# Rounding the cosine's phase by an integer conversion on ScalarE, in a long convolution followed by a gated layer

## Chip, core and metric

The kernel runs on one core of one Trainium2 chip. The metric is the time of one execution on the device in microseconds (us). Several runs of the same kernel are compared by their median.

## What is computed

The reference has two halves. The first is a long convolution along the sequence, for 4 batches of 12480 positions and 128 channels; the second sends every one of the 49920 rows through a layer with 2048 hidden units, whose gate is a cosine.

```python
def _attn_ref(x, v, pos_emb, w1, w2):           # x, v: (4, 12480, 128)
    h_mlp = np.maximum(pos_emb @ w1, 0.0) @ w2
    window = np.exp(-0.01 * np.arange(S))[:, None]
    h_filt = h_mlp * window
    u = x * v
    L = 2 * S
    Uf = np.fft.rfft(u, n=L, axis=1)
    Hf = np.fft.rfft(h_filt, n=L, axis=0)
    y = np.fft.irfft(Uf * Hf[None, :, :], n=L, axis=1)[:, :S, :]
    return (x * y).astype(np.float32)

def _moe_ref(x, w_in, w_out):                   # x: (49920, 128)
    h = x @ w_in                                # (128, 2048)
    g = h * np.cos(h)
    return (g @ w_out).astype(np.float32)       # (2048, 128)
```

All of it is float32; the two weights of the second half arrive as float64.

## The kernel before

**The convolution.** The transform over the sequence is written as matmuls of a two-stage factorisation (96 by 120). For each batch there are five stages: `u` (load x and v, multiply, sums and differences of mirrored positions, into the big buffer `slots`), `f1` (first forward matmuls), `f2` (second forward matmuls and the product with the filter's spectrum), `i1` (first inverse matmuls) and `i2` (second inverse matmuls, then the product with x and a store of the result to DRAM as `zd`). A stage is a generator that yields after every small unit of work, with a number that says how many steps of the second half should go by before the next unit.

**The stage u.** `u_load` issues two DMAs for one group of positions, into tiles `xt` (3 buffers) and `vt` (2 buffers). `u_multiply` (L395) multiplies `xt` by `vt` in two halves of 256 elements in 104 partitions; the engine of each half is chosen by a function that the caller gives. `u_sums` (L401) writes the sum of the halves (on GpSimd) and their difference (on VectorE) into `slots`. There are 30 groups in a batch. The groups of batch b + 1 run inside the stage `i2` of batch b (`inverse_units`), once `i2` has read the places in `slots` that they overwrite. In batch 0's `i2`, a quarter of the multiplications run on GpSimd and the rest on VectorE; in the later ones all run on VectorE. The groups of batch 0 run at the start of the kernel, with a choice of engines of their own.

**The second half.** It runs from about 340 us to the end, woven into the convolution of all later stages. One step is one tile of up to 128 rows by 4 (512 columns) and one of the 16 blocks of 128 hidden units: 98 tiles of rows by 16 blocks, 1568 steps. `moe_up` does the first matmul into the PSUM tile `ph` (TensorE, L743), then `a` = ph / (2 pi) + 1/4 on ScalarE (L746), `k` = a rounded to a whole number on VectorE, by adding and subtracting a large constant (L749), and `f` = a - k on GpSimd (L752). `moe_act`, one step later, does the sine of 2 pi f on ScalarE (`cs`, L757), which is cos(h), and `gt` = ph * cs on VectorE (L759). `moe_down`, four steps later, adds the second matmul into the accumulator `acc` (L768; in every second tile near the end the accumulator is called `cv`). `ph` has 4 PSUM buffers, so the matmul of a step needs the `gt` of four steps before. `a` has 3 buffers, `k` and `f` 2.

Each tile of rows is loaded from `zd` (tile `zb`), turned by four transposes (L126) and copied by ScalarE (`at`, L737). At the end of a tile, ScalarE evicts `acc` (`ot`, L774), four transposes and a copy (`ob`, L783) follow, and SP issues the stores to the output (L794).

**The order.** The schedule is written out by hand: the text of the program decides the order of the instructions on each engine. The main loop goes over the steps; after each step it draws units of convolution until they cover what is owed:

```python
            owed += 1.0
            while owed > 0.0:
                owed -= next(conv, owed)
```

All loads and stores are issued by SP's queue, in the program's order. In the stage `i2` a group's matmuls (L504) use a table `tm` (2 buffers, loaded at L676) and x again (`xs`); the eviction with the product is `zs` on VectorE (L511).

**The weights.** They are converted from the bits of float64 to float32 beside the stages f1 and i1 of batch 0: `convert_units` goes over pieces, `float32_parts` (two activations with a scale among others) and `float32_join` do one.

Of the kernel before, what the change touches and what calls it, by code (L numbers as in the profile page):

```python
# [8 lines left out]

F32 = mybir.dt.float32  # L10
U32 = mybir.dt.uint32
AF = mybir.ActivationFunctionType
ALU = mybir.AluOpType
# [3 lines left out]
P = 128  # L17
BANK = 512
DECAY = -0.01

INV_TWO_PI = 1.0 / (2.0 * math.pi)

TWO_PI = 6.283185

ROUND = 12582912.0

TAPS = 10400

# [2 lines left out]
def kernel(  # L31
# [46 lines left out]
    nc = tc.nc  # L78
# [9 lines left out]
    ODD = 64  # L88
# [12 lines left out]
    UA = 2  # L101
# [7 lines left out]
    dram = ctx.enter_context(tc.tile_pool(name="dram", bufs=1, space=DRAM))  # L109
    hd = dram.tile([N1 // 2, N2, 2, CB, 4], F32, name="hd")  # L110
    zd = dram.tile([NROWS, G, D], F32, name="zd")
    wd = dram.tile([N1 // 2, KE, 2, N2], F32, name="wd")
    td = dram.tile([N2 // G, N1, G, 2, R], F32, name="td")
    wind = dram.tile([D, DFF], F32, name="wind")
    csd = dram.tile([N2, 2, N2], F32, name="csd")
# [10 lines left out]
        nc.tensor.transpose(dst, src, ident[0:n, 0:n])  # L126


    def float32_parts(pool, raw):
        lo, hi = raw[:, :, 0], raw[:, :, 1]  # L130

        power = pool.tile([P, WCOL], U32, name="power", bufs=2)
        nc.vector.tensor_scalar(out=power[:, :], in0=hi, scalar1=20, scalar2=0x7FF,
                                op0=ALU.logical_shift_right, op1=ALU.bitwise_and)
        nc.gpsimd.tensor_scalar(out=power[:, :], in0=power[:, :], scalar1=1023.0 - 127.0,
                                scalar2=0.0, op0=ALU.subtract, op1=ALU.max)
        nc.gpsimd.tensor_scalar(out=power[:, :], in0=power[:, :], scalar1=255.0,
                                scalar2=float(1 << 23), op0=ALU.min, op1=ALU.mult)

        sig = pool.tile([P, WCOL], U32, name="sig", bufs=2)  # L140
        nc.vector.tensor_scalar(out=sig[:, :], in0=hi, scalar1=0xFFFFF, scalar2=0x100000,
                                op0=ALU.bitwise_and, op1=ALU.bitwise_or)
        high = sig[:, :].bitcast(F32)
        nc.scalar.activation(high, sig[:, :], AF.Copy, scale=2.0 ** -20)
        low = pool.tile([P, WCOL], F32, name="low", bufs=1)
        nc.scalar.activation(low[:, :], lo, AF.Copy, scale=2.0 ** -52)
        nc.gpsimd.tensor_tensor(high, high, low[:, :], op=ALU.add)
        return power, high

    def float32_join(dst, raw, power, high):  # L150
# [6 lines left out]
        if dst.space == DRAM:  # L157
# [9 lines left out]
    def convert_units(pool, pieces):  # L167

        raws, half = [], None
        for i in range(len(pieces) + 1):  # L170
            while len(raws) < min(i + 2, len(pieces)):
                raws.append(pool.tile([P, WCOL, 2], U32, name="raw", bufs=3))
                nc.sync.dma_start(raws[-1][:, :, :], pieces[len(raws) - 1][1])
            yield
            if i > 0:
                float32_join(pieces[i - 1][0], raws[i - 1], *half)
            if i < len(pieces):
                half = float32_parts(pool, raws[i])


    class Tables:
# [212 lines left out]
        xt, vt = tiles  # L394
        engine.tensor_tensor(xt[:, half, :], xt[:, half, :], vt[:, half, :], op=ALU.mult)  # L395

    def u_sums(u, tiles, a):
        both = tiles[0][:, :, :].rearrange("p h (n b i) -> p h n b i", n=UA, i=2)
        below, above = both[:, 0, ::-1, :, :], both[:, 1, :, :, :]
        for place, op, e in ((a, ALU.add, nc.gpsimd), (ODD + a, ALU.subtract, nc.vector)):  # L400
            e.tensor_tensor(u[0:R, :, place:place + UA, :].transpose([0, 2, 1, 3]),  # L401
                            below, above, op=op)

# [158 lines left out]
    def u_units(b, bufs, u, engine, side="left"):  # L562

        with tc.tile_pool(name="xv", bufs=bufs, side=side) as pool:
            tiles = {}

            def before(j):
                tiles[j] = u_load(pool, bufs, b, j * UA)

            def after(j, _):  # L570
                for half in range(2):
                    u_multiply(tiles[j], half, engine(j, half))
                    yield
                if j == H // UA - 2:
                    clear_gap(u)
                u_sums(u, tiles.pop(j), j * UA)
                yield

            yield from units(H // UA, U_STEPS, before, lambda j, ps, i: None, after, 3,
                             ahead=bufs - 2)  # L580
# [159 lines left out]
    def moe_up(pool, n, c):  # L740
        m = G * rows_of(n)
        ph = ps_h.tile([P, BANK], F32, name="ph")
        nc.tensor.matmul(ph[:, 0:m], w_in_sb[:, c * P:(c + 1) * P], ats[n][:, 0:m],  # L743
                         start=True, stop=True)
        a = pool.tile([P, BANK], F32, name="a", bufs=3)
        nc.scalar.activation(a[:, 0:m], ph[:, 0:m], AF.Identity,  # L746
                             bias=quarter[:, 0:1], scale=INV_TWO_PI)
        k = pool.tile([P, BANK], F32, name="k")
        nc.vector.tensor_scalar(out=k[:, 0:m], in0=a[:, 0:m], scalar1=ROUND,  # L749
                                scalar2=ROUND, op0=ALU.add, op1=ALU.subtract)  # L750
        f = pool.tile([P, BANK], F32, name="f")
        nc.gpsimd.tensor_tensor(f[:, 0:m], a[:, 0:m], k[:, 0:m], op=ALU.subtract)  # L752
        return ph, f, m

    def moe_act(pool, ph, f, m):
        cs = pool.tile([P, BANK], F32, name="cs")
        nc.scalar.activation(cs[:, 0:m], f[:, 0:m], AF.Sin, scale=TWO_PI)  # L757
        gt = pool.tile([P, BANK], F32, name="gt", bufs=4)
        nc.vector.tensor_tensor(gt[:, 0:m], ph[:, 0:m], cs[:, 0:m], op=ALU.mult)  # L759
        return gt  # L760
# [39 lines left out]
    with tc.manual_schedule():  # L800
        with tc.tile_pool(name="psum", bufs=8, space=PSUM) as psum, \
# [71 lines left out]

            backs = [inverse_units(lambda: bank(), b) for b in range(B)]

            def beside(units, pieces, more=lambda pool: iter(())):
                with tc.tile_pool(name="convert", bufs=1) as pool:
                    convert, other = convert_units(pool, pieces), more(pool)
# [8 lines left out]
            beside(f1_units(bank, slots[0:R, :, :, :], 0.55),  # L887
                   [(wind[:, c], w) for c, w in in_pieces])
# [7 lines left out]
            wpool = ctx.enter_context(tc.tile_pool(name="weights", bufs=1))  # L896
# [10 lines left out]
            beside(i1_units(bank), [(w_out_sb[:, c, :], w) for c, w in out_pieces], some_groups)  # L907
# [97 lines left out]
```

## Time and profile before

| what | value |
|---|---|
| time, median of 3 runs | 3761.64 us (3761.51 to 3764.51) |
| profiled execution, first to last instruction | 3758.9 us; no time of its own stands beside this span |
| TensorE (PE) busy | 3690.6 us, 98% |
| VectorE (DVE) busy | 2773.7 us, 74% |
| ScalarE (ACT) busy | 2508.2 us, 67% |
| GpSimd (POOL) busy | 2557.6 us, 68% |
| mean granted clock of TensorE | 0.995 of full speed |
| x * v on VectorE, L395 | 177 times, 132.6 us, mean 751 ns |
| x * v on GpSimd, L395 | 63 times, 50.5 us, mean 812 ns |
| difference on VectorE, L401 | 120 times, 72.2 us, mean 601 ns |
| sum on GpSimd, L401 | 120 times, 108.8 us, mean 906 ns |

In a group's row of the profile stand the line, the engine, the operation, what is written and read with the shape of one instruction and their number, then the busy time in us and the mean duration of one in ns, and after the next bar the time for which the engine stood idle just before them with what ended it. A line of waits names who waited, what it waited for, the sum in us, how often, and the longest. A line of the timeline has the start and the duration in us; an idle time of the engine before it stands in brackets.

### The profile page before, as it was taken

The numbers are of one execution on the slowest core, as the hardware profiler recorded it, in microseconds if no ns is written. First come the engines' busy times: TensorE is split into PE (matmuls) and PEld (weight loads), VectorE is DVE, ScalarE is ACT, GpSimd is POOL, SyncE is SP. The second block draws the span as 40 slices with busy tenths as digits, with TensorE's granted clock in tenths as the row PEclk, the third lists the DMA queues.
The fourth block names the chain that finished last, engine by engine and source line by source line (L and its number), as shares of the span: only waits on it lengthen the run. The fifth ranks groups of instructions, "written<-read, shape, count | busy, mean of one in ns | idle before, by whom it ended". The sixth has DMA issues, their size and how long they took to land.

```text
span 3758.9 us, 47177 instructions
## 1 busy us (share of the span) xinstructions
PE 3690.6 (98%) x13546; PEld 2110.4 (56%) x13546; DVE 2773.7 (74%) x5586; ACT 2508.2 (67%) x4660; POOL 2557.6 (68%) x2318
## 2 busy tenths in 40 slices
PE   7898999999999999999999999999999999999999
PEld 6777555555566556555565556555566544444444
DVE  8887997687866787788766776788765666666666
ACT  5757776766665557766665567666664677777777
POOL 6666776588845665688745664788644677777776
PEclk9999999999999999999999999999999999999999
DMA  6263551022203650122104530122105200000000
GB/s 167 64 185 107 155 167 33 25 72 79 72 12 91 181 151 12 40 79 77 52 18 128 180 105 21 52 79 76 38 21 172 76 23 17 17 23 18 17 23 13
DMA packets 209499, 276.14 MB, mean 73 GB/s; under 512 B 17111, under 2 KB 146535, under 8 KB 209111
## 3 DMA queue, kind: packets, MB, share of 16 engines
q1 hardware_dynamic: 209239, 273.12, 24.8%
q8 instruction: 109, 1.79, 0.2%
q14 instruction: 151, 1.24, 0.1%
HBM read 193.64 MB, written 79.42 MB: 73 GB/s over the span
## 4 chain that ended last, share of the span: by engine, by line
PE 88%; DVE 3%; POOL 3%; ACT 2%; DMA 2%; issue 1%; SPq 0%; POOLq 0%; DVEq 0%; ACTq 0%
PE ph L743 33%; PE acc L768 28%; PE cv L504 5%; PE cv L768 5%; PE cv L479 4%; PE cv L407 3%; PE cv L448 3%; PE ph L126 2%; POOL f L752 1%; PE ps L407 1%; PE ps L448 1%; DMA tm<-td 1%; DMA wd<-w 1%; ACT cs L757 1%; DVE k L749 1%
## 5 line engine op out<-in xcount | busy, mean ns | idle before, releaser
L752 POOL TENSOR_TENSOR f<-a,k 128x512 f32<-128x512 f32 (+1 forms) x1568 | 1986.2, 1267 | 1060.5 <-DVE k L749 1059.1
L743 PE MATMUL ph<-at,w_in_sb 128*128 128x512 f32 (+1 forms) x3136 | 1599.0, 591 | 3.7 <-DVE gt L759 2.7
L746 ACT ACTIVATE a<-ph,quarter 128x512 f32<-128x512 f32 (+1 forms) x1568 | 1071.2, 683 | 704.8 <-PE ph L743 695.2
L768 PE MATMUL acc<-gt,w_out_sb 128*128 128x512 f32 (+1 forms) x2688 | 1370.3, 591 | 0.0
L759 DVE TENSOR_TENSOR gt<-ph,cs 128x512 f32<-128x512 f32 (+1 forms) x1568 | 1077.3, 687 | 359.9 <-ACT cs L757 341.8
L757 ACT ACTIVATE cs<-f 128x512 f32<-128x512 f32 (+1 forms) x1568 | 981.0, 626 | 366.6 <-POOL f L752 364.3
L749 DVE TENSOR_SCALAR k<-a 128x512 f32<-128x512 f32 (+1 forms) x1568 | 792.9, 506 | 550.7 <-ACT a L746 524.2
L768 PEld LDWEIGHTS acc<-gt,w_out_sb 128*128 128x128 f32 x2688 | 508.4, 189 | 642.8 <-issue 631.9
L743 PEld LDWEIGHTS ph<-at,w_in_sb 128*128 128x128 f32 x3136 | 553.2, 190 | 337.7 <-issue 257.5
L474 POOL TENSOR_TENSOR slots<-slots,t 120x256 f32<-120x256 f32 x384 | 312.9, 821 | 59.9 <-DVE t L467 25.6
L504 PEld LDWEIGHTS cv<-slots,tm 96*104 96x104 f32 x1920 | 238.6, 169 | 106.8 <-issue 85.4
L504 PE MATMUL cv<-slots,tm 96*104 96x128 f32 x1920 | 251.7, 273 | 9.9 <-POOL tm L297 5.0
L768 PE MATMUL cv<-gt,w_out_sb 128*128 128x512 f32 (+1 forms) x448 | 224.5, 583 | 1.0 <-DVE gt L759 1.0
L479 PEld LDWEIGHTS cv<-cs,slots 120*96 120x96 f32 x1536 | 176.7, 167 | 67.2 <-issue 65.2
L479 PE MATMUL cv<-cs,slots 120*96 120x120 f32 x1536 | 183.2, 266 | 0.0
L448 PEld LDWEIGHTS cv<-slots,w 124*120 124x120 f32 x576 | 103.7, 184 | 124.3 <-issue 112.3
L407 PEld LDWEIGHTS cv<-c,slots 104*124 104x124 f32 x768 | 132.6, 192 | 72.2 <-issue 60.0
L448 PE MATMUL cv<-slots,w 124*120 124x256 f32 x576 | 173.0, 380 | 0.0
L407 PE MATMUL cv<-c,slots 104*124 104x192 f32 x768 | 151.8, 327 | 5.4 <-DVE gt L759 3.5
L768 PEld LDWEIGHTS cv<-gt,w_out_sb 128*128 128x128 f32 x448 | 84.9, 190 | 104.8 <-issue 99.5
L489 DVE TENSOR_TENSOR slots<-cv,other 96x240 f32<-96x240 f32 x384 | 133.1, 394 | 1.5 <-ACT other L487 1.4
L395 DVE TENSOR_TENSOR xt<-xt,vt 104x256 f32<-104x256 f32 x177 | 132.6, 751 | 0.6 <-DMA vt<-in_v_dram 0.6
(131 smaller groups left out, 2520.9 us busy)
## 6 DMA issues: line engine op xcount, KB each, us to landing
h<-hd SPq DMA_DIRECT2D x144, 240.0 KB
tm<-td SPq DMA_DIRECT2D x96, 312.0 KB
xt<-in_x_dram SPq DMA_DIRECT2D x120, 208.0 KB
vt<-in_v_dram SPq DMA_DIRECT2D x120, 208.0 KB
xs<-in_x_dram SPq DMA_DIRECT2D x120, 208.0 KB
zd<-zs SPq DMA_DIRECT2D x119, 208.0 KB
zb<-zd SPq DMA_DIRECT2D x96, 256.0 KB
w<-wd SPq DMA_DIRECT2D x144, 116.2 KB
```

The lines of the kernel that those rows point to most:

```text
L407: nc.tensor.matmul(ps[0:KE, i * 2 * N1:(i + 1) * 2 * N1], u[:, b, 0:KE, i], c1[0:u.shape[0], :, :].rearrange("p r k -> p (r k)"), start=Tr ...
L448: nc.tensor.matmul(pi, w[:, i, :], parts[0:KE, :, k], start=True, stop=True)
L474: nc.gpsimd.tensor_tensor(y[:, r], y[:, r], t[:, r], op=op)
L479: nc.tensor.matmul(ps[0:N1, (i * 2 + r) * N2:(i * 2 + r + 1) * N2], parts[0:N2, r, :, b, i], cs[:, r, :], start=True, stop=True)
L504: nc.tensor.matmul(ps[0:R, i * D:(i + 1) * D], t[:, i, r, :], slots[0:N1, :, place, :], start=(r == 0), stop=(r == 1))
L743: nc.tensor.matmul(ph[:, 0:m], w_in_sb[:, c * P:(c + 1) * P], ats[n][:, 0:m], start=True, stop=True)
L746: nc.scalar.activation(a[:, 0:m], ph[:, 0:m], AF.Identity, bias=quarter[:, 0:1], scale=INV_TWO_PI)
L749: nc.vector.tensor_scalar(out=k[:, 0:m], in0=a[:, 0:m], scalar1=ROUND, scalar2=ROUND, op0=ALU.add, op1=ALU.subtract)
L752: nc.gpsimd.tensor_tensor(f[:, 0:m], a[:, 0:m], k[:, 0:m], op=ALU.subtract)
L757: nc.scalar.activation(cs[:, 0:m], f[:, 0:m], AF.Sin, scale=TWO_PI)
L759: nc.vector.tensor_tensor(gt[:, 0:m], ph[:, 0:m], cs[:, 0:m], op=ALU.mult)
L768: nc.tensor.matmul(accs[n][:, 0:m], w_out_sb[:, c, :], gt[:, 0:m], start=(c == 0), stop=(c == NFC - 1))
```

## The change

In each step, `a` is gone. ScalarE adds a constant number of quarter turns to `ph` and writes `k` as an int32, so that its conversion does the rounding. VectorE then forms `f` = (ph + constant) - k, reading `ph` from PSUM again and `k` as an integer. The division by 2 pi is in the first weight, and the factor 2 pi that `gt` then lacks is in the second; both come from the scales of the activations that convert the weights. The constant goes round 0.25, 0.75, -0.25 and -0.75 with the block, and the sign of the sine's scale goes with it. `k` keeps 2 buffers, `f` has 3. The constant tile `quarter` is gone.

The groups of u for batches 1 to 3 multiply on GpSimd alone, and their sum and their difference both run on GpSimd. Those of batch 0 stay as they were.

```diff
+TURNS = ((0.25, 1.0), (0.75, -1.0), (-0.25, -1.0), (-0.75, 1.0))
...
-    def float32_parts(pool, raw):
+    def float32_parts(pool, raw, factor):
...
-        nc.scalar.activation(high, sig[:, :], AF.Copy, scale=2.0 ** -20)
+        nc.scalar.activation(high, sig[:, :], AF.Copy, scale=factor * 2.0 ** -20)
...
-        nc.scalar.activation(low[:, :], lo, AF.Copy, scale=2.0 ** -52)
+        nc.scalar.activation(low[:, :], lo, AF.Copy, scale=factor * 2.0 ** -52)
...
-    def u_sums(u, tiles, a):
+    def u_sums(u, tiles, a, takers):
...
-        for place, op, e in ((a, ALU.add, nc.gpsimd), (ODD + a, ALU.subtract, nc.vector)):
+        for place, op, e in ((a, ALU.add, takers[0]), (ODD + a, ALU.subtract, takers[1])):
...
-                u_sums(u, tiles.pop(j), j * UA)
+                u_sums(u, tiles.pop(j), j * UA, (nc.gpsimd, nc.gpsimd if b else nc.vector))
...
-                      lambda j, half: nc.gpsimd if b == 0 and j % 2 > half else nc.vector,
+                      lambda j, half: nc.gpsimd,
...
-        a = pool.tile([P, BANK], F32, name="a", bufs=3)
-        nc.scalar.activation(a[:, 0:m], ph[:, 0:m], AF.Identity,
-                             bias=quarter[:, 0:1], scale=INV_TWO_PI)
-        k = pool.tile([P, BANK], F32, name="k")
-        nc.vector.tensor_scalar(out=k[:, 0:m], in0=a[:, 0:m], scalar1=ROUND,
-                                scalar2=ROUND, op0=ALU.add, op1=ALU.subtract)
-        f = pool.tile([P, BANK], F32, name="f")
-        nc.gpsimd.tensor_tensor(f[:, 0:m], a[:, 0:m], k[:, 0:m], op=ALU.subtract)
-        return ph, f, m
+        k = pool.tile([P, BANK], I32, name="k")
+        nc.scalar.activation(k[:, 0:m], ph[:, 0:m], AF.Identity, bias=TURNS[c % 4][0])
+        f = pool.tile([P, BANK], F32, name="f", bufs=3)
+        nc.vector.scalar_tensor_tensor(out=f[:, 0:m], in0=ph[:, 0:m],
+                                       scalar=TURNS[c % 4][0], in1=k[:, 0:m], op0=ALU.add, op1=ALU.subtract)
+        return ph, f, m, TURNS[c % 4][1] * TWO_PI
...
-        nc.scalar.activation(cs[:, 0:m], f[:, 0:m], AF.Sin, scale=TWO_PI)
+        nc.scalar.activation(cs[:, 0:m], f[:, 0:m], AF.Sin, scale=scale)
...
-            quarter = wpool.tile([P, 1], F32, name="quarter")
-            nc.vector.memset(quarter[:, :], 0.25)
```

The two calls that convert the weights give `INV_TWO_PI` and `2.0 * math.pi` as the factor.

More of the change, by code (lines that the diff above doesn't have):

```diff
@@ L10 @@
 F32 = mybir.dt.float32
+I32 = mybir.dt.int32
 U32 = mybir.dt.uint32
@@ L165, with convert_units @@
                   for c in range(0, NFC, WCOL // D)]
-    def convert_units(pool, pieces):
+    def convert_units(pool, pieces, factor):
         raws, half = [], None
@@ L177, in convert_units @@
             if i < len(pieces):
-                half = float32_parts(pool, raws[i])
+                half = float32_parts(pool, raws[i], factor)
     class Tables:
@@ L744, in moe_up, with moe_act @@
                          start=True, stop=True)
-        a = pool.tile([P, BANK], F32, name="a", bufs=3)
-        nc.scalar.activation(a[:, 0:m], ph[:, 0:m], AF.Identity,
-                             bias=quarter[:, 0:1], scale=INV_TWO_PI)
-        k = pool.tile([P, BANK], F32, name="k")
-        nc.vector.tensor_scalar(out=k[:, 0:m], in0=a[:, 0:m], scalar1=ROUND,
-                                scalar2=ROUND, op0=ALU.add, op1=ALU.subtract)
-        f = pool.tile([P, BANK], F32, name="f")
-        nc.gpsimd.tensor_tensor(f[:, 0:m], a[:, 0:m], k[:, 0:m], op=ALU.subtract)
-        return ph, f, m
-    def moe_act(pool, ph, f, m):
+        k = pool.tile([P, BANK], I32, name="k")
[4 more added lines that the diff above has]
+        return ph, f, m, TURNS[c % 4][1] * TWO_PI
+    def moe_act(pool, ph, f, m, scale):
         cs = pool.tile([P, BANK], F32, name="cs")
-        nc.scalar.activation(cs[:, 0:m], f[:, 0:m], AF.Sin, scale=TWO_PI)
+        nc.scalar.activation(cs[:, 0:m], f[:, 0:m], AF.Sin, scale=scale)
         gt = pool.tile([P, BANK], F32, name="gt", bufs=4)
@@ L874, with beside @@
             backs = [inverse_units(lambda: bank(), b) for b in range(B)]
-            def beside(units, pieces, more=lambda pool: iter(())):
+            def beside(units, pieces, factor, more=lambda pool: iter(())):
                 with tc.tile_pool(name="convert", bufs=1) as pool:
-                    convert, other = convert_units(pool, pieces), more(pool)
+                    convert, other = convert_units(pool, pieces, factor), more(pool)
                     for i, _ in enumerate(units):
@@ L887 @@
             beside(f1_units(bank, slots[0:R, :, :, :], 0.55),
-                   [(wind[:, c], w) for c, w in in_pieces])
+                   [(wind[:, c], w) for c, w in in_pieces], INV_TWO_PI)
             lpool = ctx.enter_context(tc.tile_pool(name="late", bufs=1))
@@ L903 @@
             w_out_sb = wpool.tile([P, NFC, D], F32, name="w_out_sb")
-            quarter = wpool.tile([P, 1], F32, name="quarter")
-            nc.vector.memset(quarter[:, :], 0.25)
             nc.sync.dma_start(w_in_sb[:, :], wind[:, :])
-            beside(i1_units(bank), [(w_out_sb[:, c, :], w) for c, w in out_pieces], some_groups)
+            beside(i1_units(bank), [(w_out_sb[:, c, :], w) for c, w in out_pieces], 2.0 * math.pi,
+                   some_groups)
         ps_acc = ctx.enter_context(tc.tile_pool(name="ps_acc", bufs=1, space=PSUM))
```

## The prediction

> **What bounds the kernel now.** I read the page first: one engine is busy nearly all the time, and the five operations of a step of the second half stand among the costliest groups.
>
> ```profile
> PE 3690.6 (98%) x13546; PEld 2110.4 (56%) x13546; DVE 2773.7 (74%) x5586; ACT 2508.2 (67%) x4660; POOL 2557.6 (68%) x2318
> ...
> L752 POOL TENSOR_TENSOR f<-a,k 128x512 f32<-128x512 f32 (+1 forms) x1568 | 1986.2, 1267 | 1060.5 <-DVE k L749 1059.1
> ...
> L746 ACT ACTIVATE a<-ph,quarter 128x512 f32<-128x512 f32 (+1 forms) x1568 | 1071.2, 683 | 704.8 <-PE ph L743 695.2
> ...
> L759 DVE TENSOR_TENSOR gt<-ph,cs 128x512 f32<-128x512 f32 (+1 forms) x1568 | 1077.3, 687 | 359.9 <-ACT cs L757 341.8
> L757 ACT ACTIVATE cs<-f 128x512 f32<-128x512 f32 (+1 forms) x1568 | 981.0, 626 | 366.6 <-POOL f L752 364.3
> L749 DVE TENSOR_SCALAR k<-a 128x512 f32<-128x512 f32 (+1 forms) x1568 | 792.9, 506 | 550.7 <-ACT a L746 524.2
> ```
>
> TensorE sets the end. What the other engines do matters only where TensorE stands still for them, so the second view is TensorE's waits from 340 us on, where the steps begin (the 50 us that it idles before that lie in stages whose work does not change).
>
> ```profile
> PE cv L504 <- DMA tm<-td: 4.8, 6, 1.4
> PE cv L407 <- DVE gt L759: 3.5, 3, 1.9
> PE ph L743 <- DVE gt L759: 2.7, 5, 0.8
> PE cv L407 <- DVE slots L417: 1.9, 2, 1.0
> PE cv L768 <- DVE gt L759: 1.0, 2, 0.7
> PE ph L743 <- ACT at L737: 0.6, 1, 0.6
> PE ph L126 <- ACT ot L774: 0.5, 1, 0.5
> ```
>
> Columns: total us, times, longest. The sum is 15.0 us in 20 waits. A 512-column matmul is drawn 0.59 us long while the next follows after 0.43 (pairs start 0.86 apart in the timeline), so each wait lost 0.16 us more than shown: 15.0 + 20 x 0.16 = 18.2 us. The timeline of the second row's longest wait shows one more loss:
>
> ```profile
> 591.51 1.02 PE L768 MATMUL acc<-gt,w_out_sb 128*128 128x512 f32 x2
> ...
> 592.23 0.72 POOL L395 TENSOR_TENSOR xt<-xt,vt 104x256 f32<-104x256 f32 x1
> 593.03 1.30 POOL L401 TENSOR_TENSOR slots<-xt 104x256 f32<-104x256 f32 x1
> ...
> 594.26 1.57 DVE L749 TENSOR_SCALAR k<-a 128x512 f32<-128x512 f32 x1
> ...
> 594.38 0.78 PE L407 MATMUL cv<-c,slots 104*124 104x192 f32 x2 [1.85 <-DVE gt L759]
> ```
>
> TensorE was free at 592.37 and started at 594.38, when the last sum of the next batch's x * v was there. The granted clock then reads 0.50 from 595 to 598: the matmuls of about 3.4 us take twice their time, 1.7 us lost. So all that a change to the other engines can win is 18.2 + 1.7 = 19.9 us, 0.5%. The third view, busy time by stage, tells whether TensorE stays the bound:
>
> ```profile
> 735.00:1020.00 285.00, 285.00 (x808) 145.03 (x807) 230.49 (x459) 188.94 (x300) 247.92 (x229) 1.00 0.26 75
> 1178.00:1383.00 205.00, 203.35 (x854) 119.42 (x853) 156.72 (x278) 113.04 (x185) 130.33 (x111) 1.00 0.59 177
> 2946.00:3734.00 788.00, 788.00 (x2003) 359.89 (x2003) 507.78 (x891) 613.29 (x973) 564.51 (x445) 1.00 0.07 19
> ```
>
> Columns: stretch, PE, PEld, DVE, ACT, POOL, clock, DMA. The rows are the f2 stage (137 steps), the i2 stage with x * v (85 steps) and the end, steps alone (445).
>
> **The change, part by part.** As built, TensorE's and SP's instructions and ScalarE's places stand in the same order in both kernels; VectorE has one instruction for one in the steps.
>
> ScalarE: k for a, one for one, both 512 elements out of PSUM. What is new is the integer output and constants in place of a pointer bias. Below: the plain copy from PSUM of this size, 0.574 (at, L737); above: a itself, 0.683. An integer input cost nothing in L144 (256 elements, 0.417). I take 0.60, near the copy. ScalarE falls by up to 1568 x 0.11 = 171 us and is not the bound anywhere (613 of 788 at most), so this gains nothing by itself.
>
> VectorE: f from PSUM and an integer tile for k at 0.506. The nearest row is gt, as long and also with one operand in PSUM: 0.687. A scalar_tensor_tensor on integers (L151, 256 elements) took 0.418, the two-operand ops on PSUM of that size 0.412, so neither form nor type shows a charge; the widest shown for that form is L293, 0.420 for 208 elements, some 0.05 over gt's line. f is thus 0.69 to 0.74. I take 0.69: +0.18 a step, 1568 x 0.18 = 284 us. Off VectorE go 165 multiplications at 0.75 (124 us) and 90 subtractions at 0.60 (54 us). Sum: 2774 + 284 - 178 = 2880 us, 77%. What covers it is TensorE, stage by stage. f2, the tightest: 230.5 less its 137 k (83.0, as they run 0.60 each there) plus 137 x 0.69 = 242 of 285. i2: 156.7 - 38.3 (k) - 41.3 - 10.8 (x * v) + 58.7 = 125 of 205. End: 507.8 - 201.4 + 307 = 613 of 788. Nowhere does VectorE pass TensorE, so +284 us cost nothing; were the cover gone, each 0.1 us would cost 41 us in the three f2 stages.
>
> GpSimd: 1986 us of f go, 165 x 0.81 + 90 x 0.91 = 216 us come: 2558 - 1986 + 216 = 788 us, 21%. It has no work of the steps left, so nothing of theirs is queued behind x * v, and x * v behind none of theirs.
>
> A step's chain was 0.68 + 0.51 + 1.27 + 0.63 + 0.69 = 3.78 us and becomes 0.60 + 0.69 + 0.63 + 0.69 = 2.61. It lies beside four steps of matmuls, so this too pays only where TensorE waits. Two weights' factors and the dropped fill of quarter cost nothing: the scale stands in activations that are there already.
>
> Now the waits, one by one. **cv L407 <- gt** (3.5 + 3 x 0.16 = 4.0, and 1.7 of clock): the last x * v before f1. In the first of them its last vt load was issued at 584.64, when VectorE, queued behind steps, had finished an older multiplication at 584.58. Loads of this kind landed after 3.05 to 4.92 us in the chain of waits, so at 587.7 to 589.6; two multiplications and two sums on GpSimd take 2 x 0.81 + 2 x 0.91 = 3.44 us: 591.1 to 593.0, against 592.4 when TensorE wants it; and the load itself will go sooner. Of 5.7 us I take 5.5, at least 3. **cv L407 <- slots L417** (2.2): a VectorE eviction right after that, behind k of 1.57 us beside a GpSimd f (0.41 where it runs alone). f will read one tile of SBUF and one of PSUM, as gt does, whose longest is 0.694; I take 1.5, between 0 and 2.2. **ph L743 <- gt** (2.7 + 0.8 = 3.5): banks of four steps before, held by the chain that loses 1.2 us; 2.5, between -1 (VectorE's queue is fuller in f2) and 3.5. **cv L768 <- gt** (1.3): the last steps, one after the other; the 352-wide f on GpSimd takes 0.93, and f on VectorE 0.52 with no k between: 1.0. **tm <- td** (4.8 + 6 x 0.16 = 5.8): a load on SP's queue. In the i2 stage SP stood 85.8 us for VectorE's xt L395, that is for a multiplication to free vt's buffer, and behind it stand the output stores and the zb load, then xs and tm. In two of the six waits (tm issued at 1222.50 and 1336.99, landed after 5.24 and 5.67 us) four and three other transfers left right ahead of tm, all released by the vt load. If GpSimd multiplies as the data land, vt, stores and zb leave about 3 us sooner and tm finds the queues free. Against that, zs, which releases xs ahead of tm, comes 0.2 us later behind a longer f, and vt now travels with zd and xt. Between -5 and 5.8; I take 3.5. **at, ot** (1.4): untouched.
>
> Sum: 5.5 + 1.5 + 2.5 + 1.0 + 3.5 = 14.0 us. The profiled execution's span is 3758.9, 2.7 under the median of the runs, 3761.6; both drop alike: 3745 and 3747.6, say 3748. A difference under 0.2% (7.5 us) cannot be told from none here.
>
> **Two rules weighed.** Row: the multiplication of 104x256 on VectorE takes 0.751 in the mean and 0.405 at best, on GpSimd 0.812 and 0.717 at best. The Trainium skill, "GPSIMD Engine Reference", section Engine selection, speaks against this move: elementwise work belongs on VectorE, GpSimd is about half as fast. By the best cases that holds, and by it the move loses 165 x 0.31 = 51 us of engine time; the rows beside the steps say 10 us, and GpSimd has 79% of the span free, so the sum is the same by either. Row: a pause of 2.0 us at 592 was followed by half the clock. The skill, "TensorE: Matmul & The Clock Gate", section Why this matters for your kernels, asks for no pause over some 3 us; by the rule this pause would not have been the cause and 1.7 us of my 14.0 could stay. I go by the row.
>
> **Rivals.** (1) No change: TensorE has 98%, and the waits only change their names: the last sum still comes late, tm is late by its transfer and not by its issue. Then the tail and a part of ph remain, 2 to 6 us: 3757. For it: six waits name a DMA. Against: the vt load's release at 584.58. Chance 0.15. (2) Slower: f on VectorE in the three f2 stages. VectorE there has 285 - (230.5 - 83.0) = 137.5 us for 137 f: from 1.00 us each it becomes the bound. At 1.05 us that is 0.05 x 411 = 21 us, less the gains 3768; at 1.27, what GpSimd took for the same subtraction, 0.27 x 411 = 111 us, and 445 x (1.27 + 0.69 - 1.77) = 85 us at the end: 3944. For it: no row has this mix of integer SBUF and float PSUM operands. Against: L151 and gt. Chance 0.09. (3) Slower by DMA: with vt beside tm, tm lands up to 1.2 us later (208 KB at 177 GB/s) in 56 loads, of which the usual ones have about as much to spare; half a microsecond over in each gives 28 us: 3776. Chance 0.04. That the change does not do what it says is excluded by the built instructions.
>
> **How the numbers follow.** Forecast 0.72, rivals 0.15, 0.09 and 0.04. Lowest: all 19.9 us gone, 3741.7, with the scatter of the runs 3740. Upwards the range takes in the whole first rival, 3764, and leaves out the slower two. Faster 0.72, same 0.15, slower 0.13.
>
> **What would show it.** f near 0.69 and k near 0.60; VectorE about 77%, GpSimd about 21%; cv L407 <- gt gone from TensorE's waits, no clock of 0.50 at 595; tm at most 2 us. Wrong: f over 1.00, VectorE over 95% in the f2 stage, TensorE's waits above 15 us, or the clock falling elsewhere.

## The result and the profile after

The changed kernel takes 3738.06 us (median of 4 runs, 3736.99 to 3740.27). The kernel before, run beside it, takes 3763.07 us (4 runs, 3761.51 to 3765.24). The ratio is 0.9937, with an interval of 0.9922 to 0.9951: 25.0 us less. The profiled spans are 3758.9 and 3734.9 us, 24.0 apart; the profiled run of the kernel after took 3736.99 us. The forecast was 3748 in a range of 3740 to 3764. The sign was right, and the time lies 2 us below the range.

The page of the kernel after, its first row and the step's four operations with the new x * v:

```profile
PE 3681.9 (99%) x13546; PEld 2109.8 (56%) x13546; DVE 2805.7 (75%) x5330; ACT 2294.6 (61%) x4660; POOL 714.6 (19%) x1005
...
L749 ACT ACTIVATE k<-ph 128x512 int32<-128x512 f32 (+1 forms) x1568 | 932.8, 595 | 1237.0 <-PE ph L746 1236.5
L751 DVE SCALAR_TENSOR_TENSOR f<-ph,k 128x512 f32<-128x512 f32 (+1 forms) x1568 | 1080.1, 689 | 792.8 <-ACT k L749 779.5
...
L759 DVE TENSOR_TENSOR gt<-ph,cs 128x512 f32<-128x512 f32 (+1 forms) x1568 | 1064.1, 679 | 60.5 <-ACT cs L757 60.4
L757 ACT ACTIVATE cs<-f 128x512 f32<-128x512 f32 (+1 forms) x1568 | 973.2, 621 | 0.6 <-DVE f L751 0.6
...
L398 POOL TENSOR_TENSOR xt<-xt,vt 104x256 f32<-104x256 f32 x228 | 165.8, 747 | 514.5 <-DMA vt<-in_v_dram 513.3
```

ScalarE now waits 1237 us for TensorE (695 before). VectorE, in turn, waits for ScalarE's k, and GpSimd for the loads. Nothing in the chain of a step waits for GpSimd any more. TensorE's waits from 335 us to 3760 us, in the kernel after (us in total, times, longest):

```profile
PE cv L507 <- POOL tm L300: 5.0, 1, 5.0
PE ph L746 <- ACT at L740: 0.6, 1, 0.6
PE ph L129 <- ACT ot L774: 0.5, 1, 0.5
PE cv L507 <- DMA tm<-td: 0.2, 1, 0.2
```

The first row lies at 332 to 337 us, ahead of the steps; the kernel before has the same 5.0. In the part with steps, 15.0 us in 20 waits have become 1.3 us in 3. The stretches of the kernel after (columns as in the forecast's rows): f2, i2, the end, and last four microseconds just behind the first matmul of f1 (586.8 us), the place where before the half clock began.

```profile
726.00:1010.00 284.00, 284.00 (x805) 144.62 (x804) 238.16 (x459) 166.64 (x299) 68.14 (x92) 1.00 0.26 75
1168.00:1371.00 203.00, 202.81 (x852) 119.38 (x851) 127.20 (x200) 102.60 (x186) 79.71 (x111) 1.00 0.61 179
2924.00:3712.00 788.00, 788.00 (x2004) 359.85 (x2003) 575.76 (x891) 538.16 (x973) 0.00 (x0) 1.00 0.07 19
588.00:592.00 4.00, 4.00 (x17) 2.49 (x16) 2.92 (x7) 1.94 (x4) 0.00 (x0) 1.00 0.00 0
```

TensorE has no gap in f2, at the end and behind the start of f1, where the clock stays at 1.00; in the 203 us of i2 it lacks 0.2.

TensorE executes the same 13546 matmuls in the same order in both kernels, so the two traces can be laid beside each other one instruction at a time. The lead of the kernel after is 1.0 us at 300 us (unchanged code; this start differs by up to 5.7 us between the profiles of this document), 2.8 at 400, 9.4 at 600, 10.1 at 1200, 14.6 at 1500, 18.9 at 2200, 22.0 from 2700 to 3700, and 24.0 at the end. It grows in jumps, nearly all where TensorE started late before, and stays level elsewhere. Only one place gives back more than 0.1 us: 0.4 us at 1306 us, where the kernel after has its own wait for tm.

### The profile page after: what moved, and what is told of

It is laid out like the page before. It is cut to its first block, busy times and chain, and to the rows that moved or that the text cites. A ratio compares the mean times of both kernels' runs of the same rounds, so it can differ in the third digit from the quotient of the medians.

```text
span 3734.9 us, 46660 instructions
## 1 busy us (share of the span) xinstructions
PE 3681.9 (99%) x13546; PEld 2109.8 (56%) x13546; DVE 2805.7 (75%) x5330; ACT 2294.6 (61%) x4660; POOL 714.6 (19%) x1005
## 4 chain that ended last, share of the span: by engine, by line
PE 95%; DVE 1%; DMA 1%; ACT 1%; POOL 1%; issue 1%; SPq 0%; DVEq 0%; ACTq 0%; POOLq 0%
PE ph L746 36%; PE acc L768 31%; PE cv L507 6%; PE cv L768 5%; PE cv L482 4%; PE cv L451 3%; PE cv L410 3%; PE ph L129 2%; PE ps L410 2%; PE ps L451 1%; PE ps L482 1%; DMA wd<-w 1%; DVE slots L492 0%; PE ps L457 0%; DVE ftile L367 0%
## 5 line engine op out<-in xcount | busy, mean ns | idle before, releaser
L749 ACT ACTIVATE k<-ph 128x512 int32<-128x512 f32 (+1 forms) x1568 | 932.8, 595 | 1237.0 <-PE ph L746 1236.5
L751 DVE SCALAR_TENSOR_TENSOR f<-ph,k 128x512 f32<-128x512 f32 (+1 forms) x1568 | 1080.1, 689 | 792.8 <-ACT k L749 779.5
L768 PE MATMUL acc<-gt,w_out_sb 128*128 128x512 f32 (+1 forms) x2688 | 1369.4, 591 | 0.0
L759 DVE TENSOR_TENSOR gt<-ph,cs 128x512 f32<-128x512 f32 (+1 forms) x1568 | 1064.1, 679 | 60.5 <-ACT cs L757 60.4
L768 PEld LDWEIGHTS acc<-gt,w_out_sb 128*128 128x128 f32 x2688 | 508.0, 189 | 642.4 <-issue 630.0
L477 POOL TENSOR_TENSOR slots<-slots,t 120x256 f32<-120x256 f32 x384 | 281.1, 738 | 1149.2 <-DVE t L476 623.1
L398 POOL TENSOR_TENSOR xt<-xt,vt 104x256 f32<-104x256 f32 x228 | 165.8, 747 | 514.5 <-DMA vt<-in_v_dram 513.3
L768 PE MATMUL cv<-gt,w_out_sb 128*128 128x512 f32 (+1 forms) x448 | 224.0, 583 | 0.0
L404 POOL TENSOR_TENSOR slots<-xt 104x256 f32<-104x256 f32 x210 | 157.2, 756 | 94.1 <-PE cv L507 78.2
L768 PEld LDWEIGHTS cv<-gt,w_out_sb 128*128 128x128 f32 x448 | 85.0, 190 | 103.2 <-issue 99.5
L492 DVE TENSOR_TENSOR slots<-cv,other 96x240 f32<-96x240 f32 x384 | 132.9, 393 | 1.4 <-ACT other L490 1.1
```

Source lines behind the costliest of these rows:

```text
L477: nc.gpsimd.tensor_tensor(y[:, r], y[:, r], t[:, r], op=op)
L749: nc.scalar.activation(k[:, 0:m], ph[:, 0:m], AF.Identity, bias=TURNS[c % 4][0])
L751: nc.vector.scalar_tensor_tensor(out=f[:, 0:m], in0=ph[:, 0:m], scalar=TURNS[c % 4][0], in1=k[:, 0:m], op0=ALU.add, op1=ALU.subtract)
L768: nc.tensor.matmul(accs[n][:, 0:m], w_out_sb[:, c, :], gt[:, 0:m], start=(c == 0), stop=(c == NFC - 1))
```

## Experiments

Two theories. **The steps**: x * v and tm came late because of GpSimd's f, so taking f off GpSimd gives nearly all of the gain wherever u runs. **The move of u**: f on VectorE only shortens a chain that was hidden, and what paid was that x * v no longer stood in VectorE's queue. The kernel before ran on the same chips as each set of runs: 3759.88 us (15 runs) beside s1 to s4, 3760.65 (9) beside s5 to s7 and b1, 3759.16 (12) beside s9 to s11 and b3. With the 3763.07 beside the kernel after, it differs by 3.9 us from set to set, so a difference of that size between kernels of different sets is not shown by their times. Where it matters, the matched traces are given as well.

| kernel | us, median | ratio to before, interval |
|---|---|---|
| s1: steps changed, u as before | 3742.05 | 0.9951 (0.9937 to 0.9964) |
| s2: u changed, steps as before | 3806.80 | 1.0126 (1.0112 to 1.0140) |
| s3: before, one more buffer for vt | 3754.60 | 0.9987 (0.9978 to 0.9996) |
| s4: after, difference on VectorE | 3738.14 | 0.9940 (0.9928 to 0.9953) |
| s5: after, later u on VectorE alone | 3740.67 | 0.9947 (0.9934 to 0.9959) |
| s6: s5 with a GpSimd operation a step, free | 3781.03 | 1.0055 (1.0041 to 1.0068) |
| s10: s5 with a GpSimd operation a step, paced | 3771.86 | 1.0030 (1.0018 to 1.0042) |
| s7: after, 256 more columns a step on VectorE | 3740.96 | 0.9947 (0.9934 to 0.9959) |
| s11: after, 384 more columns a step on VectorE | 3797.14 | 1.0098 (1.0082 to 1.0113) |
| s9: after, bias by a pointer | 3737.64 | 0.9939 (0.9926 to 0.9953) |
| b1: after, no tm groups beside i1 | 3733.13 | 0.9927 (0.9914 to 0.9939) |
| b3: b1, i1's eviction shared out | 3749.88 | 0.9974 (0.9963 to 0.9985) |

**s1, the steps alone.** The kernel after with the engines of u as they were.

```diff
-                u_sums(u, tiles.pop(j), j * UA, (nc.gpsimd, nc.gpsimd if b else nc.vector))
+                u_sums(u, tiles.pop(j), j * UA, (nc.gpsimd, nc.vector))
-                      lambda j, half: nc.gpsimd,
+                      lambda j, half: nc.gpsimd if b == 0 and j % 2 > half else nc.vector,
```

> The new steps (k on ScalarE, f on VectorE), x * v with the engines of before. Theory A, each part of the change removes its own waits: the steps' part takes away TensorE's waits for gt (ph 2.7 us shown, the tail 1.0) with their hidden shares, some 8 us; x * v stays in VectorE's queue, which would be busy 178 of 189 us in batch 0's i2 and 177 of 205 in the later ones, so cv L407 <- gt (3.5 us shown) and tm <- td (4.8) stay: 3755, between 3751 and 3759, against 3763 before and 3738 after. Theory B, f on GpSimd alone held everything up, x * v included: all waits go, 3738 to 3742.

Measured: 3742.05 us, the upper end of the 3738 to 3742 of the steps theory and not 3755. Matched instruction by instruction, s1 gains 19.5 us on the kernel before after 300 us, where the kernel after gains 23.0. No wait for the last x * v is left; of tm's waits four stay, 2.5 us in all. The reason stands in the multiplications of the later batches. They are in VectorE's queue in both kernels, 160 each, first in the kernel before (shortest, median and longest in ns, then first and last start)

```profile
L395 DVE TENSOR_TENSOR xt<-xt,vt x160: 405/769/1529, 380.1 to 2230.7; 104x256 f32<-104x256 f32 x160
```

and then in s1:

```profile
L398 DVE TENSOR_TENSOR xt<-xt,vt x160: 409/416/426, 381.0 to 2216.5; 104x256 f32<-104x256 f32 x160
```

The same operation, same engine, same place: half the time, once GpSimd has no f. In the kernel before, sorted by whether a GpSimd operation overlaps, the mean is 0.821 us beside one (142 cases) and 0.412 alone (18).

**s2, u alone.** The kernel before with the new engines of u.

```diff
-        for place, op, e in ((a, ALU.add, nc.gpsimd), (ODD + a, ALU.subtract, nc.vector)):
+        for place, op, e in ((a, ALU.add, takers[0]), (ODD + a, ALU.subtract, takers[1])):
-                u_sums(u, tiles.pop(j), j * UA)
+                u_sums(u, tiles.pop(j), j * UA, (nc.gpsimd, nc.gpsimd if b else nc.vector))
-                      lambda j, half: nc.gpsimd if b == 0 and j % 2 > half else nc.vector,
+                      lambda j, half: nc.gpsimd,
```

> The old steps (f on GpSimd), x * v and both sums of batches 1 to 3 on GpSimd. Theory A: GpSimd is then over-full where x * v runs, 148.8 + 35 x 0.81 + 24 x 0.91 = 199 us of 189 in batch 0's i2, 130.3 + 53 x 0.81 + 26 x 0.91 = 197 of 205 in the later ones; slower than before, 3775, between 3766 and 3790, with waits for gt grown. Theory B, it is x * v out of VectorE's queue that wins and GpSimd has room: cv L407 <- gt and tm <- td go, 3750 to 3754.

Measured: 3806.80 us, 47 more than before; slower was expected, but not by so much. TensorE's waits in s2:

```profile
PE cv L504 <- DMA tm<-td: 17.1, 12, 2.4
PE ph L743 <- DVE gt L759: 14.0, 20, 1.9
PE cv L407 <- POOL slots L401: 9.6, 3, 3.6
```

and its two i2 stages, 376 to 580 and 1183 to 1408 us (the columns as in the rows of stretches above):

```profile
376.00:580.00 204.00, 193.98 (x752) 107.06 (x750) 163.31 (x243) 137.47 (x269) 191.93 (x194) 1.00 0.48 148
1183.00:1408.00 225.00, 217.07 (x907) 126.77 (x906) 141.47 (x218) 121.34 (x200) 191.03 (x195) 0.99 0.55 164
```

GpSimd is busy 192 of 204 us in the first: f and u queue behind each other on one engine, and the step's chain is late 20 times. Alone, then, this half of the change costs 47 us; on top of the other half it gains 3.5 us by the matched traces (23.0 against 19.5 in s1).

**s4 and s5, u on VectorE after all.** s4 puts the difference back on VectorE, s5 all of the later u, both sums included.

```diff
 s4
+                u_sums(u, tiles.pop(j), j * UA, (nc.gpsimd, nc.vector))
 s5
+                u_sums(u, tiles.pop(j), j * UA, (nc.vector if b else nc.gpsimd, nc.vector))
+                      lambda j, half: nc.vector,
```

> After, with the difference of u (L404) on VectorE again in batches 1 to 3, the multiplications and sums on GpSimd. Theory A, the multiplications are what mattered: no wait comes back over 1 us, 3738 to 3740. Rival, the difference in VectorE's queue made the last piece of x * v late: cv L410 <- gt comes back with 3 to 4 us and the half clock with it, 3741 to 3744.

> After, with all of x * v of batches 1 to 3 on VectorE: multiplications, sums and differences; GpSimd has no elementwise work in the i2 stages but batch 0's few additions for tm. Theory C, what made x * v late before was GpSimd's f, not VectorE's share: VectorE is busy some 170 of 184 us in batch 0's i2 and 164 of 203 in the later ones, still under TensorE; cv L410 <- gt stays away, tm <- td 2 to 4 us as in the run of the steps alone: 3742, between 3740 and 3746. Rival, VectorE's queue needs GpSimd's help: cv L410 <- gt returns, 3747 or more.

Measured: s4 3738.14, as the kernel after; s5 3740.67 us, 2.6 more than it. In s5 VectorE is busy 168 of 184 us in the first i2 stage, its multiplications have a median of 416 ns and a longest of 423, and TensorE's only waits that the kernel after lacks are 0.6 us more for tm. From 300 us on, the matched traces gain 22.8 us in s4 and 21.3 in s5, against 23.0 in the kernel after and 19.5 in s1; the profile of s5 reaches 300 us 2.8 us later, in unchanged code. So where u runs is worth 0 to 4 us once f has left GpSimd.

**s6 and s10, work on GpSimd that nobody needs.** To separate what GpSimd does to VectorE from what it does to the queue, s5 gets one 128x512 subtraction a step on GpSimd, whose result is not read. In s6 it depends on nothing; in s10 it reads f, so that it keeps the pace of the steps.

```diff
 s6
+        nc.gpsimd.tensor_tensor(spin[:, 1, 0:m], spin[:, 0, 0:m], spin[:, 0, 0:m], op=ALU.subtract)
 s10
+        nc.gpsimd.tensor_tensor(spin[:, 1, 0:m], f[:, 0:m], spin[:, 0, 0:m], op=ALU.subtract)
```

> The kernel with all of x * v on VectorE, and in each step one 128x512 subtraction on GpSimd, of two SBUF tiles that nothing else reads or writes (added work; no other engine waits for it). Theory D, GpSimd's f slowed VectorE's operations on two SBUF tiles by running beside them: L398 goes from 0.42 to about 0.75 us, VectorE to some 192 of 203 us in the i2 stages and over 184 in batch 0's, and TensorE's waits for x * v return: 3750, between 3746 and 3765. Rival, it was GpSimd's own queue, in which sums stood behind f: with no sum on GpSimd nothing returns, 3742, and L398 stays at 0.42.

> The kernel with all of x * v on VectorE, and in each step one 128x512 subtraction on GpSimd that reads the step's f, so that it runs once a step, as f did before (added work; its result is not used, no engine waits for it but by f's three buffers). Theory D, running beside it slows VectorE's operations on two SBUF tiles: L398 from a median of 0.42 to about 0.77 us as before the change, TensorE's waits for x * v and tm come back, some 8 to 15 us in all: 3752, between 3747 and 3762. Rival, only GpSimd's place in the step's chain did harm: 3741 to 3743, L398 at 0.42.

Measured: 3781.03 and 3771.86 us, 40 and 31 more than s5; both directions as expected, both larger than expected. In s6 GpSimd runs ahead and does its work in bunches, so that most multiplications meet none of it (median 417 ns), and 50 that do take 0.916 us in the mean. TensorE's two longest rows of waits in s6:

```profile
PE ph L746 <- DVE gt L760: 14.8, 13, 3.4
PE cv L410 <- DVE slots L404: 10.6, 3, 5.1
```

In stretches beside such waits the granted clock of s6 is half, for 20.5 us in all, so part of the 40 us is clock. In s10 the work keeps the pace of the steps. Its multiplications:

```profile
L398 DVE TENSOR_TENSOR xt<-xt,vt x175: 406/590/1462, 377.0 to 2246.0; 104x256 f32<-104x256 f32 x175
```

Beside a GpSimd operation they take 1.053 us in the mean (96 cases), alone 0.411 (79). VectorE is busy 204 of 204 us in the first i2 stage, and two of the waits of the kernel before are back and larger: ph for gt 11.4 us in 16, tm 6.8 us in 7. In s6 no data and no queue ties the added work to x * v or to the steps: its presence on GpSimd is enough to make VectorE late. In s10 there is one tie, f's three buffers, and VectorE waits for it:

```profile
DVE f L751 <- POOL spin L753: 46.2, 70, 0.9
```

All but one of these waits lie in the f2 stages and at the end, where s10 loses nothing on s5 in the matched traces. What it loses lies in the three i2 stages with x * v and up to the f1 behind them, where no such wait stands. What in the hardware the two engines share is not shown by these runs.

**s3, the reason of tm.** The kernel before, with three buffers for vt in place of two for the batches 2 and 3 (for batch 1 the third does not fit).

```diff
-        for name, src, n in (("xt", x, bufs), ("vt", v, bufs - 1)):
+        for name, src, n in (("xt", x, bufs), ("vt", v, bufs if b > 1 else bufs - 1)):
```

> Before, with a third buffer for vt in batches 2 and 3 only; nothing else. Theory A, tm is late because SP's queue stands for the multiplication that frees vt's buffer, and then sends the output stores and zb right ahead of tm: the tm <- td wait falls from 4.8 us to under 1.5, all others stay: 3758. Rival, tm is late by its own transfer, or by x * v's loads beside it: tm <- td stays at 4 to 6 us, 3763.

Measured: 3754.60 us, 5.3 less than before. Of tm's waits this is left in s3, and the other waits are the same to 0.1 us:

```profile
PE cv L504 <- DMA tm<-td: 0.5, 1, 0.5
```

This is what the forecast said of SP's queue: the vt load stood for its buffer, and the stores, zb, xs and tm stood behind it. In the kernel after, SP's waits in the second i2 stage (1168 to 1372 us) hardly name the multiplication of x * v; its sums have 4.2 us:

```profile
SPq L379 <- DVE zs L514: 125.0, 28, 6.6
SPq L379 <- POOL slots L404: 4.2, 13, 0.5
...
SPq L379 <- POOL xt L398: 0.3, 1, 0.3
```

against this in the kernel before (1178 to 1383 us):

```profile
SPq L376 <- DVE xt L395: 85.8, 27, 4.2
```

In the kernel after, a vt load follows its xt load after 0.42 us (3.5 before). At one end of a tile there, the stores and zb leave from 1207.34 to 1208.70 us, and the next tm only at 1212.44, with nothing but xs right ahead of it.

**s7 and s11, how much cover VectorE has.** The kernel after with one more VectorE multiplication a step, of ph and f into a tile that nobody reads.

```diff
 s7
+        nc.vector.tensor_tensor(spin[:, :], ph[:, 0:256], f[:, 0:256], op=ALU.mult)
 s11, m2 = min(m, 384)
+        nc.vector.tensor_tensor(spin[:, 0:m2], ph[:, 0:m2], f[:, 0:m2], op=ALU.mult)
```

> After, with one more VectorE multiplication of 256 columns in each step, one operand in PSUM, its result unused (added work; 0.41 us by the rows of that size). It stands for an f of 1.10 us. The prediction's second rival put the point from which VectorE bounds the f2 stages at 1.00 us: VectorE there 238 + 137 x 0.41 = 295 us in 284, so +11 us in each of three, nothing at the end (576 + 445 x 0.41 = 759 of 788): 3738 + 32 = 3770, between 3760 and 3785. If there is more cover than that sum says, 3738 to 3742; if VectorE is on the path everywhere, 1568 x 0.41 = 646 us more.

> After, with one more VectorE multiplication of 384 columns in each step, its result unused (added work). The one of 256 columns cost 2 to 3 us where 32 had been expected: its 0.41 us raised VectorE's busy time in the f2 stage by 38 us for 137 steps, 0.28 each, since in a full queue the next instruction starts before the last one's drawn end. By drawn durations (0.54) the f2 stages need 312 of 284 us and the end 816 of 788: 3738 + 3 x 28 + 28 = 3850. By spacing (0.41 in f2): 238 + 56 = 294 of 284 us, three times, and nothing at the end: 3738 + 33 = 3771, between 3755 and 3790.

Measured: s7 3740.96 us, 2.9 more than the kernel after (the intervals of the two ratios overlap), where some 30 more were expected; s11 3797.14, 59 more, between the two estimates. The f2 stage of s7 and then of s11:

```profile
726.00:1010.00 284.00, 284.00 (x804) 144.46 (x803) 276.20 (x597) 167.80 (x303) 66.58 (x90) 1.00 0.25 73
```

```profile
740.00:1028.00 288.00, 276.57 (x772) 138.27 (x771) 279.83 (x576) 159.62 (x287) 66.51 (x91) 1.00 0.24 73
```

At 97% both of these stages look full, and only one costs time. The rows say why. In s7, 138 operations of 0.414 us were added to the stage, which would be 57 us; VectorE's busy time rose by 38. The operations were drawn longer than the room they take: in a full queue the next one of 512 columns starts some 0.60 us after the one before, which is drawn 0.68 to 0.69. By spacing, s11 was to lose 10 us in each f2 stage; matched with the kernel after it loses 17, 16 and 15, 49 of the 60 us from 300 us on. TensorE's waits drawn in its first f2 stage, 11.5 us in 16, name two copies of ScalarE (`at` and `ob`), which itself stood idle there for 125.7 us waiting for ph. VectorE was idle for only 8 of the 288 us. That the copies are late because their engine stands behind VectorE's queue fits this, but no run shows it apart, and why it is 16 us and not 10 stays open.

**s9, the bias.** The kernel after with the four constants in a small tile, as `quarter` was.

```diff
-        nc.scalar.activation(k[:, 0:m], ph[:, 0:m], AF.Identity, bias=TURNS[c % 4][0])
+        nc.scalar.activation(k[:, 0:m], ph[:, 0:m], AF.Identity, bias=turns[:, c % 4:c % 4 + 1])
```

> After, with k's constant taken from a column of an SBUF tile, as a took it before, in place of a constant in the instruction. If k's 0.595 us against a's 0.683 come from the constant, k is 0.68 again, and the integer output costs nothing; if they come from the output or the missing scale, k stays at 0.60. In both cases ScalarE is not the bound (538 of 788 us at the end, 577 with it) and the time is 3738, within 3.

Measured: 3737.64 us, the time of the kernel after, with k in s9 at

```profile
L749 ACT ACTIVATE k<-ph,turns 128x512 int32<-128x512 f32 (+1 forms) x1568 | 1074.0, 685 | 1127.1 <-PE ph L746 1126.5
```

The 0.09 us between a (0.683) and k (0.595) is the pointer; the integer output costs nothing. And 141 us of ScalarE's time, given back, make no difference to the end that these runs can show.

**b1 and b3, a version beyond both.** The longest wait left in the kernel after from 332 us on is the 5.0 us for the tables `tm` of the first i2 stage; some of their groups are made beside i1 of batch 0. b1 makes none there. b3 also takes 14 of the 64 units of i1's eviction off VectorE, with copies by ScalarE and sums and differences by GpSimd.

```diff
 b1
-    SOME = range(2, NG, 5)
+    SOME = range(0)
 b3, where shared
+            nc.scalar.copy(out=one[:, :, :], in_=pj[:, 0])
+            one, engine = one[:, :, :], nc.gpsimd
```

> After, with no group of tm made ahead beside the i1 stage of batch 0 (SOME empty, before 6 of 30 groups): all are made in batch 0's i2. TensorE's wait of 5.0 us for tm L300, just before the steps begin, is the queue of those groups' work on ScalarE and GpSimd: it falls under 2 us, and ScalarE and VectorE have room for them in batch 0's i2 (129 + 11 and 137 + 8 of 184 us): 3733, between 3730 and 3737. Rival, the wait is the eviction of i1 itself, or the moved groups come late in i2: 3738 or more.

> The version without groups of tm made ahead, and in batch 0's i1 a quarter of the units (14 of 64) evicted by two copies on ScalarE with sum and difference on GpSimd, in place of two VectorE operations on PSUM. TensorE's wait of 4.3 us for VectorE's L492 at the end of i1 is VectorE's backlog there: it falls by 2 us or more and 3733 becomes 3730, between 3727 and 3733. Rival, GpSimd's share comes late (it has 31 of 60 us there, and 14 x 1.5 more) and TensorE waits for it: 3733 or more.

Measured: b1 3733.13 us, 27.5 less than the kernel before beside it. That is 4.9 us below the kernel after, which was not run beside it, and the intervals of their two ratios overlap. Most of the wait only changed its name, in b1 from 335 us on:

```profile
PE cv L507 <- DVE slots L492: 4.3, 1, 4.3
```

Matched with the kernel after, b1 gains 3.4 us between 300 and 400 us: nearly all of it in TensorE's waits for the same eviction (L492), most of it at 304 to 332 us, and 0.7 in the wait above. The half clock behind lasts 6.8 us in both. b3 was to take the wait for that eviction away and failed, with 3749.88 us. Its waits from 200 to 345 us:

```profile
PE ps L482 <- DVE slots L497: 12.2, 8, 2.7
```

With the shared units TensorE waits more, and mostly for VectorE's evictions still. That the shared units hold up those behind them is likely from this, but not shown.

## Why the forecast was right in sign and too small

**What bounds, and the operations.** TensorE bounds both kernels. The new operations came out as taken: k 0.595 (0.60), f 0.689 (0.69); VectorE 75% (77), GpSimd 19% (21). VectorE's stages are 238 of 284 us (242 of 285), 127 of 203 (125 of 205) and 576 of 788 (613). The last is too high because 0.69 is drawn, and in a full queue less is taken, as s7 showed.

**The sum.** From 300 us to the end the trace gains 23.0 us; the sum said 14.0. Term by term, from the matched traces (listed: what the list of waits shows, with the 0.16 and the half clock added):

| term | taken | listed | gained |
|---|---|---|---|
| cv L407 <- gt, three f1 starts, with the half clock | 5.5 | 5.7 | 4.0 + 1.7 |
| cv L407 <- slots L417 | 1.5 | 2.2 | 2.2 |
| ph L743 <- gt | 2.5 | 3.5 | 3.5 |
| tm <- td | 3.5 | 5.8 | 5.8 |
| cv L768 <- gt | 1.0 | 1.3 | 1.4 |
| all of the list | 14.0 | 18.5 | 18.6 |
| five late starts too short for the list | none | none | 1.3 |
| second matmul of a pair late, in 27 places | none | none | 2.6 |
| the kernel after's own wait for tm at 1306 us | none | none | -0.4 |
| places of at most 0.15 us, not assigned | none | none | 0.9 |

Two steps failed. The first is the discount: the sum took 14.0 of the 18.5 us that the list showed, most of it off ph (2.5 of 3.5, "VectorE's queue is fuller in f2"), tm (3.5 of 5.8) and L417 (1.5 of 2.2), for what might take a wait's place or stay of it. Next to nothing did. The 18 waits gained all that the list held, and s3 shows for tm in the batches 2 and 3 that it was one buffer. The second is the ceiling, "all that a change to the other engines can win", from which the lower end of the range came. For the waits in the list its 18.5 without at and ot was right almost to 0.1 us. But TensorE also lost time that stands in no row of the list. At 373, 577, 1389, 2042 and 3741 us it started 0.19 to 0.31 us late with only 0.03 to 0.14 us of that drawn as idle. In 27 places the second matmul of a pair came some 0.10 us later behind the first than in the kernel after. With the small places that is the other 4.4 us. The remaining 1.0 us of the spans lies before 300 us, in the chance of the start, and 1.0 more in the runs' medians is within their scatter.

**x * v.** That the last x * v before f1 would no longer be late was right, and so was the clock at 592. The reason was not. The forecast took 0.751 on VectorE against 0.812 on GpSimd as the prices of the two engines, and gave the gain to the move. The 0.751 was the price beside GpSimd's f. With f gone VectorE does it in 0.416 (s1) and GpSimd in 0.73, and the wait goes away on either engine (s5). So for this term the size was nearly right and the mechanism was not: it was f leaving GpSimd that paid, and not x * v leaving VectorE.

**The rules weighed.** The Trainium skill, "GPSIMD Engine Reference", section Engine selection, puts such work on VectorE. Its order of the two engines is borne out without f, 0.416 against 0.73 us; in the time it made no gain to follow it (s5 is 2.6 us longer, with overlapping intervals), and GpSimd had the time free. For the pause, the row was right: by the rule of some 3 us in "TensorE: Matmul & The Clock Gate", section Why this matters for your kernels, the half clock at 595 would have stayed, and it went with the pause of 1.85 us.

**The rivals.** No change: fell, since tm's wait was one of issue and not of transfer (s3). Slower by f on VectorE: f took 0.689, and the point of 1.00 us was too low by the way it was worked out. An addition of 0.41 drawn (s7; 1.10 with f) still cost next to nothing, one of 0.55 (s11; 1.23) cost 59 us. The mechanism is real, and its place is the f2 stages, with 49 of the 60 us. Slower by DMA: with vt right behind xt, 0.2 us of waits for tm is all that is left.

## What to carry to other kernels

When an engine's operations vary by a factor of two in duration for one shape, sort them by what the other engines do meanwhile before using their mean as a price; the shortest is what they cost when the neighbour is quiet. When one instruction engine sets the end and its order is fixed, match it instruction by instruction between two profiles: that gives each term of a sum its measured size, and it finds the late starts that the list of waits leaves out (4.4 of 23.0 us here). And a wait whose cause is identified should be counted whole, with a rival of its own for what may come in its place, not cut by a discount.

## What was not expected of the hardware

- VectorE's 104x256 float32 product of two SBUF tiles takes 0.41 us alone and 0.82 (before), 0.92 (s6) or 1.05 us (s10) in the mean beside a GpSimd operation, up to 1.5. gt and f, with one operand in PSUM, keep 0.68 to 0.69 in every kernel here. The k of the kernel before, which reads one tile of SBUF, is held as well: it takes 0.43 in the median and up to 1.75 beside GpSimd's f. GpSimd feels it as well: its sum L401 has a median of 917 ns in the kernel before, and 732 in s2, where VectorE does none of u.
- VectorE overlaps the end of one operation with the start of the next: starts 0.60 us apart where 0.68 to 0.69 are drawn. Its busy share of 97% can be full (s11) or not (s7).
- The half clock did not go by the length of the pause. In s2, 3.4 us of half clock followed a pause of 1.87 us at 582, and none followed pauses of 1.87 us at 1248, of 2.40 at 2242 and of 3.15 at 2277. In all these traces the clock changes only at the steps of a grid of 3.413 us, and it went with TensorE's busy share of such a stretch. From 345 us on, over all 14 profiles, full clock was followed by half in all 6 stretches with TensorE drawn busy for 44% or less, in 5 of the 7 between 44 and 48%, and in none of some 13900 above. First the stretch of the kernel before ahead of its half clock (1.56 us busy of 3.42), then the two of s2 over which the pause of 3.15 us is spread (1.73 and 1.92 of 3.40), both kept at the full clock:

```profile
591.25:594.67 3.42, 1.56 (x5) 0.50 (x5) 2.12 (x6) 1.06 (x2) 3.34 (x5) 1.00 0.02 7
```

```profile
2271.90:2275.30 3.40, 1.73 (x4) 0.42 (x3) 1.58 (x3) 1.21 (x2) 3.32 (x5) 1.00 0.02 7
2275.30:2278.70 3.40, 1.92 (x8) 1.47 (x9) 0.21 (x2) 0.71 (x2) 3.40 (x4) 1.00 0.00 0
```

So what a pause costs depends on where it falls. This is read from the traces; no run moved a pause on purpose. The two stretches of s2 with the pauses at 1248 and 2242 (1.53 and 1.54 us busy) kept the full clock and lie within 0.03 us of stretches that did not keep it, so what decides at the border is open.
